# Sums of k and v in linear attention ahead of a softplus feed-forward block: one head at a time for every batch

## The chip, the cores and the metric

The kernel runs on one core of a Trainium2 chip. The metric is the device time of one execution in microseconds (us), median of several runs; lower is better. The engines named below are TensorE (PE for its multiplications, PEld for its weight loads), VectorE (DVE), ScalarE (ACT), GpSimd (POOL) and SyncE (SP), whose queue issues the transfers.

## What is computed

The first part is a linear attention: k and v of each head are summed over the sequence into a 64 x 64 matrix, q is multiplied with it, and each row is scaled by its root mean square. The second part is a feed-forward block with softplus. `w_in` and `w_out` arrive as float64.

```python
# B = 8 batches, H = 8 heads, S = 576 positions, D = 64
kv  = np.einsum('bhsd,bhse->bhde', k, v)          # the sums of k and v
out = np.einsum('bhsd,bhde->bhse', q, kv)
rms = np.sqrt(np.mean(out * out, axis=-1, keepdims=True) + 1e-06)
x   = out / rms * g_norm                          # then (B,H,S,D) -> (4608, 512)
h   = x @ w_in                                    # 512 -> 2048
g   = np.maximum(h, 0.0) + np.log1p(np.exp(-np.abs(h)))
y   = g @ w_out                                   # 2048 -> 512
```

## The kernel before

All work is entered as tasks into a plan, which sorts them before the program is built. A task has an engine, an assumed duration in ns, the tasks that it follows, a position and the buffers that it takes and gives back. Among the tasks that could start at nearly the same time on an engine, the one with the lowest position goes first. The positions come from a list of numbers: those of the first four chunks of weights (converted at `CONVERT`, fetched at `FETCH`), leads of several loads (`EARLY`), and those of the later chunks (`LATER`).

```python
P0 = [-71.0, -4.7, -70.3, -8.7, ...]               # 40 numbers
CONVERT, FETCH, EARLY, LATER = P0[:8], P0[8:16], P0[16:27], P0[27:]
...
def x_pos(t):       # position of a tile of 128 rows
    n = t // TB
    return t * EARLY[0] + EARLY[1] if n == 0 else first_step[0, n] - (EARLY[2] if n == 1 else EARLY[3]) + t % TB
...
def x_again(ph, t):                                # a tile of x is loaded again
    pos = first_step[ph, t // TB] - EARLY[8] + 0.5 * (t % TB)
    ... load at pos - EARLY[9] ...
def leave(ph, t, bank, done, pos):                 # partial results of a former phase
    ... load at pos - EARLY[10] ...
```

The sums of one batch are made in five parts: four of 128 partitions with 4 positions each (the parts p = 0 to 3 hold heads p and p + 4), and the tail, the last 64 positions of all heads. `pairs(x, i)` is two heads side by side, 128 wide. Batches 0 and 1 (`wide_rows`) have the four main parts a head at a time (64 x 64, line 505); everything else multiplies two heads of k with two heads of v (128 x 128, line 513), and only the two diagonal blocks of the product are used later.

```python
def kv_of(b):
    pos = x_pos(first_tile[b]) - (EARLY[4] if b else EARLY[5])
    wide_rows = b < 2
    bank = slot("o")                               # one bank of PSUM
    MAIN = 4 * P
    for p in range(NP + 1):
        tail = p == NP
        ks, vs = (slot(f"tail{i}" if tail else "m") for i in range(2))
        n = S - MAIN if tail else P
        def load(src, s, ...):
            if tail: ...                           # k: two transfers (L483), v: one (L485)
            x = new(s, [P, H, D])
            src = src[b, p::NP, :MAIN].rearrange("h (s i) d -> s h i d", i=4)
            if s is ks and not wide_rows:
                for h in range(2):
                    nc.sync.dma_start(out=x[:, h::2], in_=src[:, h])                              # L491
            else:
                nc.sync.dma_start(out=x.rearrange("s (h i) d -> s h i d", h=2), in_=src)          # L493
        ...
        def run(...):
            kv = new(bank, [P, NP, 2, D]) if p == 0 else bank.tile
            for i in range(4):
                if wide_rows and not tail:
                    for e in range(2):
                        l, r = (x.tile.rearrange("s (h i) d -> s h i d", h=2)[:, e, i] for x in (ks, vs))
                        nc.tensor.matmul(kv[e * D:(e + 1) * D, p, e], lhsT=l, rhs=r, ...)         # L505
                    continue
                ...                                # l: two heads of k, r: two heads of v
                nc.tensor.matmul(kv[:, i if tail else p], lhsT=l, rhs=r, ...)                     # L513
        last = add("PE", 1640 if wide_rows and not tail else 820, run, lds + [last], pos + 0.5 * p, ...)
    # the two diagonal blocks go to kv_diag, whose other blocks stay zero (L520, L521)
```

The product with q (`o`) takes the block-diagonal `kv_diag` and so a pair of heads at a time:

```python
nc.tensor.matmul(y[r0:r0 + n, p::NP], lhsT=qT.tile[:, p, r0:r0 + n],
                 rhs=kv_diag[b % 2][:, p].rearrange("r (h d) -> r h d", d=D), ...)                # L530
```

The rows are then scaled (ACT, DVE, POOL), turned, and split into three parts of fewer bits for the feed-forward block (L437, L440, L444). That block has 192 steps, each of 12 matmuls into `h` (L668) and 9 into `s` (L675), with softplus and the split of its result between them (L688, L690, L679, L683). Where TensorE would have nothing to do before the first step, the plan puts in matmuls whose result isn't used (L784).

Of the kernel before, what the change touches and what calls it, by code (L numbers as in the profile page):

```python
# [18 lines left out]
P = 128  # L19
# [21 lines left out]
class Plan:  # L41
# [13 lines left out]
    def slot(self, ring):  # L55
        return Slot(ring)

    def add(self, engine, ns, run, after=(), pos=0.0, take=(), give=(), size=0, behind=None, follows=None):
        t = Task(engine, ns, run, [a for a in after if a is not None], pos, list(take), list(give), size)
        for s in t.give:  # L60
            s.readers += 1
        self.tasks.append(t)
        t.follows = follows
        t.behind = behind
        return t
# [77 lines left out]
def kernel(  # L143
# [24 lines left out]
    nc = tc.nc  # L168
    B, H, S, D = q.shape
# [3 lines left out]
    NP = H // 2  # L173
# [9 lines left out]
    PLACES = 8  # L183
    LAST = PHASES[-1]

    P0 = [-71.0, -4.7, -70.3, -8.7, -15.1, -0.5, -23.9, 2.7, -65.0, -28.3, -35.2, -10.7, -25.2, 1.3,
          -0.2, -2.7, 0.5, -17.5, 13.0, 9.5, 5.5, 6.5, -2.0, 2.5, 2.5, 28.0, 15.0, 14.5, 8.5, 44.5,
          49.5, 68.5, 52.5, 72.0, 94.5, 99.5, 115.5, 110.5, 114.5, 8.5]
    CONVERT, FETCH, EARLY, LATER = P0[:8], P0[8:16], P0[16:27], P0[27:]
    BY_PE = 12  # L190
    AT_ONCE = 2 * TB
# [22 lines left out]
                 h=2, o=2, tp=1, s0=1, s1=1, s2=1)  # L214
# [3 lines left out]
    slot, add = plan.slot, plan.add  # L218

    def new(s, shape, dtype=F32):  # L220
        pool = ps if s.ring in PS else sb
        s.tile = pool.tile(shape, dtype, tag=f"{s.ring}_{s.place}", name=f"{s.ring}_{s.place}")
        return s.tile

    def pairs(x, p):

        return x[:, 2 * p:2 * p + 2].rearrange("r h d -> r (h d)")


    def halves(src, e):  # L230

        return src[e * NP:(e + 1) * NP].rearrange("p s d -> s p d")
# [224 lines left out]
    kv_ready = {}  # L457
    o_tasks = {}

    def x_pos(t):  # L460

        n = t // TB
        return t * EARLY[0] + EARLY[1] if n == 0 else first_step[0, n] - (EARLY[2] if n == 1 else EARLY[3]) + t % TB

    def kv_of(b):

        pos = x_pos(first_tile[b]) - (EARLY[4] if b else EARLY[5])
        wide_rows = b < 2
        bank = slot("o")
        last = None  # L470
        MAIN = 4 * P
# [5 lines that stand above are left out]
            def load(src, s, p=p, tail=tail, n=n, ks=ks):  # L477
                if tail:
                    s.tile = tails[s is not ks]
                    src = src[b, :, MAIN:]  # L480
                    if s is ks:
                        for e in range(2):
                            nc.sync.dma_start(out=s.tile[:n, e::2], in_=halves(src, e))  # L483
                    else:
                        nc.sync.dma_start(out=s.tile[:n], in_=src.rearrange("h s d -> s h d"))  # L485
                    return
                x = new(s, [P, H, D])
                src = src[b, p::NP, :MAIN].rearrange("h (s i) d -> s h i d", i=4)
                if s is ks and not wide_rows:
                    for h in range(2):  # L490
                        nc.sync.dma_start(out=x[:, h::2], in_=src[:, h])  # L491
                else:
                    nc.sync.dma_start(out=x.rearrange("s (h i) d -> s h i d", h=2), in_=src)  # L493

            lds = [add("SP", ns, lambda src=src, s=s, load=load: load(src, s), (), pos - EARLY[6] + 0.5 * p, [s], [],
                       620 if tail else size, behind=int(pos - 2) - 3)
                   for src, s, ns, size in ((k, ks, *((500, 850) if wide_rows and not tail else (900, 1300))), (v, vs, 500, 850))]

            def run(ks=ks, vs=vs, p=p, tail=tail, n=n):
                kv = new(bank, [P, NP, 2, D]) if p == 0 else bank.tile  # L500
                for i in range(4):
                    if wide_rows and not tail:
                        for e in range(2):
                            l, r = (x.tile.rearrange("s (h i) d -> s h i d", h=2)[:, e, i] for x in (ks, vs))
                            nc.tensor.matmul(kv[e * D:(e + 1) * D, p, e], lhsT=l, rhs=r, start=(p == 0 and i == 0),  # L505
                                             stop=False, skip_group_check=True)
                        continue
                    if tail:
                        l, r = pairs(ks.tile, i), vs.tile[:, i::NP]
                    else:  # L510
                        l, r = pairs(ks.tile, i), vs.tile.rearrange("s (h i) d -> s h i d", h=2)[:, :, i]

                    nc.tensor.matmul(kv[:, i if tail else p], lhsT=l, rhs=r, start=(p == 0 and i == 0), stop=tail,  # L513
                                     skip_group_check=True)
            last = add("PE", 1640 if wide_rows and not tail else 820, run, lds + [last], pos + 0.5 * p,
                       [bank] if p == 0 else [], [ks, vs])
        kvd = kv_diag[b % 2]
        old = o_tasks.get(b - 2, [])
        kv_ready[b] = [
            add("ACT", 360, lambda: nc.scalar.copy(kvd[:D, :, :D], bank.tile[:D, :, 0]), [last] + old, pos + 2.5, [], [bank]),  # L520
            add("ACT", 360, lambda: nc.scalar.copy(kvd[D:, :, D:], bank.tile[D:, :, 1]), [last] + old, pos + 2.5, [], [bank])]  # L521

    def rows(t):
        pos = x_pos(t)
# [235 lines left out]
    for c in range(KF):  # L760
        for j in (2 * c, 2 * c + 1):
            pos = CONVERT[j] if c < 4 else LATER[c - 4] + LATER[12] * (j % 2)
            weight(j, pos, FETCH[j] if c < 4 else pos)
    for b in range(B):
        kv_of(b)
        for t in range(n_tiles):
            if parts(t)[-1][0] == b:
                rows(t)
# [51 lines left out]
```

## Time and profile before

| | |
|---|---|
| time, median of 3 runs | 917.79 us (917.73 to 917.94) |
| span of the profiled run | 917.5 us |
| last matmul ends | 913.6 us |
| sums of k and v, matmul records | 192 + 64 at 128 x 128, 128 at 64 x 64 |
| transfers | 131.44 MB in 230,386 packets, 127,408 of them under 512 bytes |

The profile gives for each engine its busy time. A group of instructions is listed as line, engine, operation, what it writes and reads, its shape and count, then total busy time in us, the mean duration in ns, and how long the engine idled before it. The durations of matmuls overlap one another, so that the time from one group's start to the next one's says more than a duration. "SPq" is the queue that issues transfers.

### The profile page before, as it was taken

The numbers are of one execution on the slowest core, as the hardware profiler recorded it, in microseconds if no ns is written. First come the engines' busy times: TensorE is split into PE (matmuls) and PEld (weight loads), VectorE is DVE, ScalarE is ACT, GpSimd is POOL, SyncE is SP. The second block draws the span as 40 slices with busy tenths as digits, with TensorE's granted clock in tenths as the row PEclk, the third lists the DMA queues.
The fourth block names the chain that finished last, engine by engine and source line by source line (L and its number), as shares of the span: only waits on it lengthen the run. The fifth ranks groups of instructions, "written<-read, shape, count | busy, mean of one in ns | idle before, by whom it ended". The sixth has DMA issues, their size and how long they took to land.

```text
span 917.5 us, 13377 instructions
## 1 busy us (share of the span) xinstructions
PE 898.1 (98%) x4863; PEld 812.4 (89%) x4863; DVE 626.6 (68%) x1055; ACT 415.1 (45%) x799; POOL 81.2 (9%) x78
## 2 busy tenths in 40 slices
PE   5799999999999999999999999999999999999998
PEld 4689999989998999999999999999999999998987
DVE  5877887875457887789856778888444455555553
ACT  4776555444334656455434455446323333333331
POOL 0324421312122100000000000000000000000000
PEclk9999999999999999999999999999999999999999
DMA  7999999397883654445433434643320433333323
GB/s 226 241 224 224 260 207 203 89 216 147 176 139 108 149 150 127 125 139 172 149 104 127 150 126 139 208 142 122 104 70 33 138 102 103 106 104 104 104 69 104
DMA packets 230386, 131.44 MB, mean 143 GB/s; under 512 B 127408, under 2 KB 204208, under 8 KB 230320
## 3 DMA queue, kind: packets, MB, share of 16 engines
q1 hardware_dynamic: 230160, 130.59, 53.7%
q8 instruction: 38, 0.62, 0.3%
q14 instruction: 28, 0.23, 0.1%
q10 hardware_dynamic: 160, 0.00, 0.0%
HBM read 91.75 MB, written 38.80 MB: 142 GB/s over the span
## 4 chain that ended last, share of the span: by engine, by line
PE 95%; DMA 2%; DVE 1%; ACT 1%; SPq 0%; issue 0%; ACTq 0%
PE s L675 44%; PE h L668 43%; PE o L530 3%; PE o L513 3%; DMA m<-in_v_dram 1%; DMA g_col<-in_g_norm_dram 1%; PE tp L547 0%; DMA tail<-in_k_dram 0%; SPq L608 0%; PE o L505 0%; PE h L367 0%; DVE xv L440 0%; DVE xv L444 0%; PE tp L585 0%; ACT L750 0%
## 5 line engine op out<-in xcount | busy, mean ns | idle before, releaser
L668 PE MATMUL h<-xv,w 128*128 128x384 f32 x2304 | 434.3, 337 | 0.9 <-ACT g L688 0.9
L675 PE MATMUL s<-w,gv 128*128 128x512 f32 x1728 | 434.2, 395 | 0.0
L668 PEld LDWEIGHTS h<-xv,w 128*128 128x128 f32 x2304 | 406.6, 188 | 15.9 <-ACT g L688 1.1
L675 PEld LDWEIGHTS s<-w,gv 128*128 128x128 f32 x1728 | 319.4, 188 | 58.9 <-issue 0.5
L688 ACT ACTIVATE g<-h 128x384 f32<-128x384 f32 x192 | 94.3, 491 | 392.7 <-PE h L668 388.2
L679 DVE TENSOR_TENSOR gv<-g,gv 128x384 fp32r<-128x384 f32 x192 | 106.4, 554 | 179.1 <-ACT gv L690 178.2
L690 ACT ACTIVATE gv<-g 128x384 fp32r<-128x384 f32 x192 | 100.9, 525 | 22.9 <-PE s L675 15.6
L683 DVE SCALAR_TENSOR_TENSOR gv<-gv 128x384 fp32r<-128x384 f32 x192 | 106.9, 557 | 6.1
L440 DVE SCALAR_TENSOR_TENSOR xv<-m,g_col,xv 128x512 fp32r<-128x512 f32 x102 | 75.9, 744 | 1.3 <-ACT xv L437 1.1
L444 DVE SCALAR_TENSOR_TENSOR xv<-xv 128x512 fp32r<-128x512 f32 x108 | 74.4, 689 | 2.6
L437 ACT ACTIVATE xv<-m,g_down 128x512 fp32r<-128x512 f32 x102 | 69.5, 710 | 1.1 <-DMA m<-x 1.1
L539 POOL TENSOR_TENSOR r<-r,half 128x8 f32<-128x8 f32 x36 | 65.5, 1818 | 3.0
L715 DVE SCALAR_TENSOR_TENSOR m<-s,scale,m 128x512 f32<-128x512 f32 x24 | 17.9, 747 | 30.1 <-PE s L675 30.1
L530 PE MATMUL o<-kv_diag,m 128*128 128x128 f32 (+1 forms) x296 | 36.9, 275 | 0.0
L530 PEld LDWEIGHTS o<-kv_diag,m 128*128 128x128 f32 (+1 forms) x296 | 35.1, 179 | 2.0 <-issue 1.0
L538 POOL TENSOR_SCALAR r<-r 128x8 f32<-128x8 f32 x36 | 15.1, 419 | 240.9 <-DVE r L535 240.6
L715 DVE SCALAR_TENSOR_TENSOR m<-s,m 128x512 f32<-128x512 f32 x36 | 23.7, 684 | 13.5 <-PE s L675 13.4
L542 DVE TENSOR_TENSOR x<-o,r 128x512 f32<-128x512 f32 x33 | 22.7, 687 | 13.5 <-POOL r L539 13.4
L535 DVE TENSOR_REDUCE r<-x 128x8 f32<-128x512 f32 x36 | 24.5, 680 | 10.2 <-ACT x L598 10.0
L303 ACT ACTIVATE sq<-sq,big 128x512 bf16<-128x512 bf16 x32 | 22.9, 717 | 11.2 <-DVE m L299 11.1
L286 ACT ACTIVATE sq<-raw 128x512 bf16<-128x512 bf16 x32 | 21.2, 664 | 12.5 <-DMA raw<-in_moe_w_in_dram 8.3
L299 DVE SCALAR_TENSOR_TENSOR m<-sq,m 128x512 f32<-128x512 bf16 x32 | 22.1, 690 | 6.3 <-ACT sq L286 4.9
(69 smaller groups left out, 452.8 us busy)
## 6 DMA issues: line engine op xcount, KB each, us to landing
m<-x SPq DMA_DIRECT2D x102, 256.0 KB, 4.7
part<-m SPq DMA_DIRECT2D x72, 256.0 KB, 2.7
m<-part SPq DMA_DIRECT2D x72, 256.0 KB, 3.7
raw<-in_moe_w_in_dram SPq DMA_DIRECT2D x16, 512.0 KB, 5.7
m<-in_v_dram SPq DMA_DIRECT2D x32, 256.0 KB, 4.2
raw<-in_moe_w_out_dram SPq DMA_DIRECT2D x16, 512.0 KB, 5.1
qa<-in_q_dram SPq DMA_DIRECT2D x24, 288.0 KB, 6.3
m<-in_k_dram SPq DMA_DIRECT2D x48, 128.0 KB, 4.1
```

The costliest lines, as they stand in the source:

```text
L437: nc.scalar.activation(cols(0, F32R), x.tile, func=AF.Identity, scale=g_down)
L440: nc.vector.scalar_tensor_tensor(out=cols(1, F32R), in0=x.tile, scalar=g_col, in1=cols(0), op0=ALU.mult, op1=ALU.subtract)
L444: nc.vector.scalar_tensor_tensor(out=cols(2, F32R), in0=cols(1), scalar=-RADIX, in1=cols(0), op0=ALU.mult, op1=ALU.add)
L530: nc.tensor.matmul(y[r0:r0 + n, p::NP], lhsT=qT.tile[:, p, r0:r0 + n], rhs=kv_diag[b % 2][:, p].rearrange("r (h d) -> r h d", d=D), start= ...
L539: nc.gpsimd.tensor_tensor(out=r.tile, in0=r.tile, in1=half, op=ALU.pow)
L668: nc.tensor.matmul(hp, lhsT=w_in.tile[:, i, kd * P:(kd + 1) * P], rhs=xv.tile[:, i, kd], start=(m == 0), stop=(m == 3 * KD - 1))
L675: nc.tensor.matmul(mine[i].tile, lhsT=gv.tile[:, m, i * P:(i + 1) * P], rhs=w_out.tile[:, m], start=(c == cs[0] and m == 0), stop=(c == cs ...
L679: nc.vector.tensor_tensor(out=gv.tile[:, 1], in0=g.tile, in1=gv.tile.bitcast(F32)[:, 0], op=ALU.subtract)
L683: nc.vector.scalar_tensor_tensor(out=gv.tile[:, 2], in0=f32[:, 1], scalar=-RADIX, in1=f32[:, 0], op0=ALU.mult, op1=ALU.add)
L688: a = add("ACT", 490, lambda: nc.scalar.activation(new(g, [P, NT]), h.tile, func=AF.Softplus, scale=1.0 + E), [a], s, [g], [h])
L690: a = add("ACT", 530, lambda: nc.scalar.activation(new(gv, [P, 3, NT], F32R)[:, 0], g.tile, func=AF.Copy, scale=DOWN), [a], s, [gv])
L715: a = add("DVE", 700, lambda: nc.vector.scalar_tensor_tensor(out=new(ot, [P, d_model]), in0=bank.tile, scalar=(scale if ph == LAST else 1. ...
```

## The change

Every batch gets its sums one head at a time, tails too; the wide form goes away. A matmul then makes only the 64 x 64 product that is used, and two heads that write the two halves of the partitions follow each other. The sums of a pair need only one 64-wide column in PSUM instead of two. As k no longer has to lie with two heads side by side, it is loaded as v is: one transfer a part, in runs of 4 positions (1 KB), and the tail of k in one transfer too. The product with q stays with pairs of heads. The plan's assumed durations follow, and the list of positions is chosen anew.

```diff
-    P0 = [-71.0, -4.7, -70.3, -8.7, -15.1, -0.5, -23.9, 2.7, -65.0, -28.3, -35.2, -10.7, -25.2, 1.3,
-          -0.2, -2.7, 0.5, -17.5, 13.0, 9.5, 5.5, 6.5, -2.0, 2.5, 2.5, 28.0, 15.0, 14.5, 8.5, 44.5,
-          49.5, 68.5, 52.5, 72.0, 94.5, 99.5, 115.5, 110.5, 114.5, 8.5]
+    P0 = [-72.5, -0.2, -57.8, -8.7, -11.6, -12.0, -21.4, 2.2, -57.5, -32.8, -36.2, -10.7, -28.2, 0.3,
+          -3.2, -2.2, 0.5, -17.5, 12.5, 9.5, 5.5, 6.5, -2.0, 2.5, 2.5, 33.5, 12.5, 14.5, 8.5, 44.5,
+          49.5, 68.5, 52.5, 73.0, 96.5, 99.5, 115.5, 110.5, 114.5, 8.5]
@@ kv_of, loads
-                    if s is ks:
-                        for e in range(2):
-                            nc.sync.dma_start(out=s.tile[:n, e::2], in_=halves(src, e))
-                    else:
-                        nc.sync.dma_start(out=s.tile[:n], in_=src.rearrange("h s d -> s h d"))
+                    nc.sync.dma_start(out=s.tile[:n], in_=src[b, :, MAIN:].rearrange("h s d -> s h d"))
                     return
-                ... (two transfers of k for batches 2 to 7, as shown above)
+                nc.sync.dma_start(out=new(s, [P, 2, 4, D]), in_=src[b, p::NP, :MAIN].rearrange("h (s i) d -> s h i d", i=4))
@@ kv_of, matmuls
-                kv = new(bank, [P, NP, 2, D]) if p == 0 else bank.tile
+                kv = new(bank, [P, NP, D]) if p == 0 else bank.tile
                 for i in range(4):
-                    ... (both forms, as shown above)
+                    for e in range(2):
+                        l, r = (x.tile[:, i + e * NP] if tail else x.tile[:, e, i] for x in (ks, vs))
+
+                        nc.tensor.matmul(kv[e * D:(e + 1) * D, i if tail else p], lhsT=l, rhs=r,
+                                         start=(p == 0 and i == 0), stop=tail, skip_group_check=True)
-            last = add("PE", 1640 if wide_rows and not tail else 820, run, lds + [last], pos + 0.5 * p,
-                       [bank] if p == 0 else [], [ks, vs])
+            last = add("PE", 600, run, lds + [last], pos + 0.5 * p, [bank] if p == 0 else [], [ks, vs])
@@ kv_of, copies to kv_diag: the same two, from bank.tile[r:r + D]
```

More of the change, by code (lines that the diff above doesn't have):

```diff
@@ L467, in kv_of @@
         pos = x_pos(first_tile[b]) - (EARLY[4] if b else EARLY[5])
-        wide_rows = b < 2
         bank = slot("o")
@@ L479, in load @@
                     s.tile = tails[s is not ks]
-                    src = src[b, :, MAIN:]
-                    if s is ks:
-                        for e in range(2):
-                            nc.sync.dma_start(out=s.tile[:n, e::2], in_=halves(src, e))
-                    else:
-                        nc.sync.dma_start(out=s.tile[:n], in_=src.rearrange("h s d -> s h d"))
-                    return
-                x = new(s, [P, H, D])
-                src = src[b, p::NP, :MAIN].rearrange("h (s i) d -> s h i d", i=4)
@@ L489, in load @@
[L489 to L497, printed above, removed]
@@ L499, in run @@
-            def run(ks=ks, vs=vs, p=p, tail=tail, n=n):
-                kv = new(bank, [P, NP, 2, D]) if p == 0 else bank.tile
-                for i in range(4):
[L502 to L514, printed above, removed]
@@ L515, in kv_of @@
-            last = add("PE", 1640 if wide_rows and not tail else 820, run, lds + [last], pos + 0.5 * p,
-                       [bank] if p == 0 else [], [ks, vs])
+                    nc.sync.dma_start(out=s.tile[:n], in_=src[b, :, MAIN:].rearrange("h s d -> s h d"))
+                    return
+                nc.sync.dma_start(out=new(s, [P, 2, 4, D]), in_=src[b, p::NP, :MAIN].rearrange("h (s i) d -> s h i d", i=4))
+            lds = [add("SP", 500, lambda src=src, s=s, load=load: load(src, s), (), pos - EARLY[6] + 0.5 * p, [s], [],
+                       650 if tail else 850, behind=int(pos - 2) - 3) for src, s in ((k, ks), (v, vs))]
@@ new lines, in run @@
+            def run(ks=ks, vs=vs, p=p, tail=tail):
+                kv = new(bank, [P, NP, D]) if p == 0 else bank.tile
+                for i in range(4):
+                    for e in range(2):
+                        l, r = (x.tile[:, i + e * NP] if tail else x.tile[:, e, i] for x in (ks, vs))
+                        nc.tensor.matmul(kv[e * D:(e + 1) * D, i if tail else p], lhsT=l, rhs=r,
+                                         start=(p == 0 and i == 0), stop=tail, skip_group_check=True)
@@ L517, in kv_of @@
+            last = add("PE", 600, run, lds + [last], pos + 0.5 * p, [bank] if p == 0 else [], [ks, vs])
         kvd = kv_diag[b % 2]
[L518 to L521, printed above, removed]
+        kv_ready[b] = [add("ACT", 360, lambda r=r: nc.scalar.copy(kvd[r:r + D, :, r:r + D], bank.tile[r:r + D]),
+                           [last] + o_tasks.get(b - 2, []), pos + 2.5, [], [bank]) for r in (0, D)]
```

## The prediction

> **What bounds the kernel now.** I read the page first, then busy time by stretch, then the order of instructions on TensorE, then the transfers. The page's totals and its chain of waits come first:
>
> ```profile
> PE 898.1 (98%) x4863; PEld 812.4 (89%) x4863; DVE 626.6 (68%) x1055; ACT 415.1 (45%) x799; POOL 81.2 (9%) x78
> ...
> PE 95%; DMA 2%; DVE 1%; ACT 1%; SPq 0%; issue 0%; ACTq 0%
> ```
>
> TensorE is busy for 98% of the span and holds 95% of the chain that ends last. An average can hide a stage with another limit, so I look at stretches. The columns are the stretch, its length, then busy time and count of PE, PEld, DVE, ACT and POOL, the clock, the DMA share and GB/s:
>
> ```profile
> 0.00:10.00 10.00, 4.78 (x20) 3.12 (x22) 3.45 (x10) 2.22 (x3) 0.69 (x6) 1.00 0.75 233
> 10.00:20.00 10.00, 6.03 (x64) 4.53 (x62) 7.55 (x13) 7.04 (x14) 0.00 (x0) 1.00 0.75 205
> 20.00:30.00 10.00, 8.65 (x71) 6.95 (x70) 8.93 (x16) 8.27 (x18) 2.93 (x4) 1.00 0.99 279
> 30.00:40.00 10.00, 7.31 (x86) 5.99 (x86) 8.41 (x15) 7.69 (x16) 4.90 (x5) 1.00 0.95 227
> 40.00:50.00 10.00, 8.44 (x56) 7.09 (x54) 5.86 (x10) 5.52 (x11) 0.93 (x1) 1.00 0.84 218
> 50.00:60.00 10.00, 9.32 (x64) 8.38 (x63) 8.46 (x15) 6.48 (x15) 2.41 (x2) 1.00 0.90 242
> 60.00:70.00 10.00, 10.00 (x75) 9.49 (x74) 8.31 (x15) 7.81 (x15) 3.47 (x4) 1.00 1.14 193
> ...
> 100.00:150.00 50.00, 50.00 (x292) 45.73 (x291) 42.71 (x73) 28.16 (x55) 12.59 (x11) 1.00 0.97 216
> ```
>
> There are two regimes. Up to about 54 us TensorE has gaps (its last wait before the steady part ends at 53.27 us), while the DMA share is mostly 0.8 to 1.0 and DVE and ACT are each busy for 7 to 9 us of every 10 between 10 and 40 us. From there to 913.6 us TensorE has no gap at all: every row after 60 shows a full 10.00 or 50.00. So **in the second regime time is the sum of TensorE's work**, and a microsecond less of it is a microsecond off the end, unless something else starts to arrive late. In the first regime time is set by loads and by the chain through DVE and ACT.
>
> Which TensorE work does the change touch? Only the sums of k and v. These are the groups by shape; the number ahead of the comma is busy time with overlaps counted once, the next is the mean duration of a record:
>
> ```profile
> L513 PE MATMUL o<-m,m 128*128 128x128 f32 x192 | 24.9, 275 | 0.7 <-DMA m<-in_v_dram 0.7
> L513 PE MATMUL o<-tail,tail 128*128 128x128 f32 x64 | 8.9, 283 | 0.0
> L505 PE MATMUL o<-m,m 128*64 128x64 f32 x128 | 7.0, 272 | 6.8 <-DMA m<-in_v_dram 6.8
> ```
>
> Each fp32 matmul leaves two records: 6 batches x 4 x 4 = 96 matmuls give 192. The kernel already holds both forms. L505, used for batches 0 and 1, is the form that the change puts everywhere: eight 64-wide matmuls a quarter instead of four 128-wide ones of which half the product is unused. So its price can be read off, as long as its early and cold executions are told from its later ones. TensorE in order of time (start, duration, group):
>
> ```profile
> 17.17 1.98 PE L505 MATMUL o<-m,m 128*64 128x64 f32 x32
> ...
> 27.04 0.69 PE L505 MATMUL o<-m,m 128*64 128x64 f32 x16
> 27.65 1.16 PE L530 MATMUL s<-kv_diag,m 128*128 128x128 f32 x8
> ...
> 51.10 1.06 PE L513 MATMUL o<-m,m 128*128 128x128 f32 x8
> 51.99 0.60 PE L585 MATMUL tp<-ident_r,m 128*128 128x128 f32 x4
> ```
>
> From the start of a group to the start of the next one: **0.61 us** for the 64-wide quarter (27.65 - 27.04), **0.89 us** for the 128-wide one (51.99 - 51.10). The chain of waits agrees, with "PE o L513 x8" at 0.89 us a group throughout.
>
> **What the Trainium skill says.** "TensorEngine Tiling (Array Packing)", Overview and Tiling Modes: a 128x64 arrangement gives two tiles that load weights and multiply in parallel, worth up to twice the speed where the stationary side is at most 64 wide; but changing the arrangement drains TensorE. The trace agrees with both halves. Eight matmuls take 0.61 us or 76 ns each, against 0.89 / 4 = 222 ns for a 128-wide one; with half the columns and no overlap, one would expect 111 ns. And the full factor is not there: by columns alone eight at 222 / 4 would be 0.44 us, and they take 0.61, which leaves some 0.17 us a group for starts and changes of arrangement.
> "TensorE: Matmul & The Clock Gate", Part 1: after idling, TensorE runs at half rate until it has been kept busy. Here the two quarters at 17.17 us take 1.91 us to the next start, so 0.95 each, against 0.61 later. That is why I don't use the mean of L505.
> "DMA: Bandwidth & Descriptors", Specifications: pieces under 512 bytes stay below line rate. Whole transfers of k in 256-byte runs (128 KB each) land in a median of 4.1 us, those of v in 1 KB runs (256 KB) in 4.2: half the bytes in the same time. The trace agrees, though both also wait behind other transfers.
>
> **The change, part by part.**
> 1. *Main sums of batches 2 to 7.* Six batches x 4 quarters = 24 groups go from 0.89 to 0.61 us: 0.28 less each. The first two (51.10 and 53.27) lie where TensorE still waits for transfers, so I count 22: 22 x 0.28 = **6.2 us**.
> 2. *Tail sums.* One group of four 128-wide matmuls per batch becomes eight 64-wide ones. Those of batches 0 and 1 (19.67 and 37.98 us) lie in the early regime; six count: 6 x 0.28 = **1.7 us**.
> 3. *Weight loads.* They double in number but are half as wide: L505's load at 158 ns median and L513's at 192 overlap their matmuls. They are already in the 0.61; nothing extra.
> 4. *Copies out of PSUM.* Two copies of 64x256 per batch before and after (353 and 369 ns). Only the stride of the source changes: nothing. They lie on ACT, which is busy 56% in 100 to 150 us.
> 5. *Loads of k, batches 2 to 7.* Two issues of 128 KB in 256-byte runs become one of 256 KB in 1 KB runs. On the queue a pair takes 1.25 us to issue, one load of v 0.45 to 0.57:
>
> ```profile
> 48.04 1.22 SPq L491 DMA_DIRECT2D m<-in_k_dram  x2
> 49.37 0.56 SPq L493 DMA_DIRECT2D m<-in_v_dram  x1
> ```
>
> So about 0.7 us of issue is saved for each of 24 loads, and 0.85 for each tail of k (1.47 for two becomes about 0.61). After 60 us that is hidden: TensorE waits for no transfer there. From 13 to 54 us the queue issues almost without a pause, and the change takes away two tails (1.7 us) and two or three loads of k (1.4 to 2.1 us), over 3 us of issue. But part of an issue's length is the queue being full, and the chain in that stretch also runs through DVE, ACT and the landing of v. I take a third: **1.2 us** off the start of the steady part.
> 6. *Positions chosen anew.* They move the conversions and fetches of the first four weight chunks, the lead of the second block (13.0 to 12.5), and the lead of later loads (28.0 to 33.5, 15.0 to 12.5). They add no instruction. They can move the start of the steady part by a microsecond or two either way. I presume that they were picked for this order of work, and credit **0.6 us**.
>
> Sum: 6.2 + 1.7 + 1.2 + 0.6 = 9.7 us; 917.8 - 9.7 = 908.1. I state **908.3 us**, a fraction kept back for hand-overs in which DVE becomes the later one.
>
> **The rivals.**
> *DVE takes the place of TensorE.* In 100 to 150 us DVE is busy for 42.7 of 50 us, 85%, with the same work to do in less time: 13 groups x 0.28 = 3.6 us fewer in the 90 us after 60 raises that to about 89%. Against it: no wait of TensorE for DVE after 54 us. For it: the order on each engine is fixed, so that one late result stops TensorE. If it bites, half the gain of parts 1 and 2 is lost: 912 to 913 us.
> *Each change of arrangement costs more among the big matmuls.* My 0.61 us is from a group between fp32 groups; in the steady part most neighbours are L668 and L675, in another type. After an L513 group the following L668 chain piece is 2.11 instead of 2.08 us, so a switch of that kind costs little today. A further 0.15 us a group would be 28 x 0.15 = 4.2 us: 912.5. For the opposite case: compared by durations (1.06 against 0.69), a group saves 0.37 us, which makes 28 x 0.37 = 10.4 instead of 7.9 and the time 906.
> *The start decides.* TensorE idles for 19.4 us in the whole span, 3.9 of them after the last matmul, and runs 9.0 us of pure warming (L784). Those and the half-rate stretch are what the start could give. If 256-byte runs and issues truly hold up the start, it could gain 4 us: 905. If the new positions starve it (the first weight fetches are moved by 1 to 7 positions, one conversion by 12), it could lose 4: 913.
> *The transfers were what mattered, and the matmuls are hidden.* Then only part 5 would show, and the time would be about 916. The rows of 10.00 after 60 us speak against it.
>
> **Range and chances.** Parts 1 and 2 give 5 to 10.4 us, the start -4 to +4, and these are independent: 8 in 10 lie within about 5 us of the middle, 903.5 to 913.5. Two per cent is 18.4 us, below 899.4 or above 936.1. Faster by that needs parts 1 and 2 at their best and 8 us from the start, of which it shows about 25 at all: 0.02. Slower by that needs a new stall that the steady part has no trace of: 0.02. Within 2%: 0.96.
>
> **What would show it.** Right: the 256 128-wide records of the sums (192 + 64) are gone and there are 8 batches x 5 groups x 16 = 640 of the 64-wide kind in place of 128; groups at about 0.61 us from start to start in 100 to 280 us; TensorE without gaps from before 54 us; and 24 loads x 1024 runs of 256 bytes become 24 x 256 of 1 KB, so that 24,576 fewer packets lie under 512 bytes and 18,432 fewer in all. Wrong: quarters at 0.75 us and over among L668 and L675 (dear switches); new waits of TensorE for DVE after 60 us; or a first steady stretch that begins more than 3 us earlier or later.

## The result, and the profile after

The changed kernel takes **912.56 us** (912.22 to 913.73, 4 runs) against 917.87 us: ratio 0.9942, 95% interval 0.9925 to 0.9960, a gain of 5.3 us. Predicted were 908.3 us, in a range of 903.5 to 913.5. A second, later measurement gave 0.9944 (0.9931 to 0.9956). The profiled execution of the kernel before was 1.4 us longer than that kernel's median, so the two spans, 917.5 and 910.9 us, differ by more than the medians do.

From the page of the changed kernel, totals and chain of waits:

```profile
PE 898.6 (99%) x5134; PEld 802.6 (88%) x5134; DVE 625.7 (69%) x1055; ACT 414.9 (46%) x799; POOL 80.6 (9%) x78
...
PE 97%; ACT 1%; DVE 1%; DMA 1%; issue 0%; ACTq 0%; DVEq 0%
```

TensorE's busy time has not fallen at all, though the sums need less of it. The groups by shape show where it went:

```profile
L494 PE MATMUL o<-m,m 128*64 128x64 f32 x512 | 22.6, 239 | 3.9 <-DMA m<-in_v_dram 3.9
L762 PE MATMUL h<-ident_r 128*128 128x512 f32 x36 | 15.7, 554 | 1.6 <-DVE ident_r L731 1.6
...
L494 PE MATMUL o<-tail,tail 128*64 128x64 f32 x128 | 5.5, 228 | 0.0
```

The sums went from 40.8 us (three groups) to 28.1, but the matmuls put in to keep TensorE warm went from 21 to 36 (9.0 to 15.7 us). They fill gaps at the start, where the new order leaves TensorE fewer waits: its idle time in the span falls from 19.4 to 12.3 us. These busy times overlap between groups and so don't add up. Counted from each group's start to the next start, without waits, the sums take 8.1 us less (33.8 to 25.7), the warming matmuls 6.2 more, and the steps of the feed-forward block, whose work is unchanged, 1.9 more. Waits fall by 7.3 us, so that waits and warming together, which is what the start could give, fall by 1.1. Stretches of the start (columns as in the prediction):

```profile
30.00:40.00 10.00, 9.39 (x119) 7.07 (x118) 9.10 (x16) 7.70 (x16) 4.59 (x5) 1.00 0.83 214
40.00:50.00 10.00, 9.74 (x72) 8.52 (x68) 9.24 (x16) 9.12 (x19) 4.69 (x4) 1.00 1.03 301
50.00:60.00 10.00, 10.00 (x98) 8.28 (x97) 8.49 (x15) 6.92 (x14) 2.41 (x2) 1.00 0.98 264
```

From 41 us on TensorE has no gap (before: 53.27). The counts came as foretold: 640 records of the narrow kind, 25,087 packets fewer under 512 bytes and 18,941 fewer in all. The tell-tale of the sums is in TensorE in order of time (start, duration):

```profile
53.69 0.69 PE L494 MATMUL o<-m,m 128*64 128x64 f32 x16
54.31 0.98 PE L653 MATMUL s<-w,gv 128*128 128x512 f32 x3
55.21 0.69 PE L494 MATMUL o<-m,m 128*64 128x64 f32 x16
55.83 0.97 PE L653 MATMUL s<-w,gv 128*128 128x512 f32 x3
...
63.32 1.05 PE L508 MATMUL o<-kv_diag,m 128*128 128x128 f32 x8
64.13 0.93 PE L653 MATMUL s<-w,gv 128*128 128x512 f32 x3
64.90 0.60 PE L525 MATMUL tp<-ident_r,x 128*128 128x128 f32 x4
```

A narrow group takes 0.61 or 0.62 us to the next start, as predicted. But three L653 behind it take 0.90 (55.21 - 54.31), and the same three behind a wide group 0.77 (64.90 - 64.13). **Part of the price of a narrow group is booked on its neighbours.** From one narrow group to the next it is 1.52 us; less three L653 at a ninth of 2.09 each, that leaves 0.82 us a group. The chain of waits shows the same. Each piece in it is counted from the end of the piece ahead (start, length). Before:

```profile
265.06 0.89 PE o L513 x8
265.95 2.08 PE s L675 x9
```

After:

```profile
258.24 0.61 PE o L494 x16
258.85 2.28 PE s L653 x9
```

The group became 0.28 us shorter, just as predicted, and the nine matmuls behind it 0.20 us longer, with no wait of TensorE there. A single narrow group is worth 0.08 us.

### The profile page after: what moved, and what is told of

Same layout as the page of the kernel before. It is cut to its first block, busy times and chain, and to the rows that moved or that the text cites. A ratio compares the mean times of both kernels' runs of the same rounds, so it can differ in the third digit from the quotient of the medians.

```text
span 910.9 us, 13889 instructions
## 1 busy us (share of the span) xinstructions
PE 898.6 (99%) x5134; PEld 802.6 (88%) x5134; DVE 625.7 (69%) x1055; ACT 414.9 (46%) x799; POOL 80.6 (9%) x78
## 4 chain that ended last, share of the span: by engine, by line
PE 97%; ACT 1%; DVE 1%; DMA 1%; issue 0%; ACTq 0%; DVEq 0%
PE h L646 44%; PE s L653 44%; PE o L508 3%; PE o L494 2%; DMA g_col<-in_g_norm_dram 1%; PE tp L563 1%; PE h L762 1%; PE tp L525 0%; PE h L367 0%; PE s L508 0%; PE h L366 0%; DVE xv L440 0%; DVE m L351 0%; ACT L728 0%; ACT L727 0%
## 5 line engine op out<-in xcount | busy, mean ns | idle before, releaser
L653 PE MATMUL s<-w,gv 128*128 128x512 f32 x1728 | 434.1, 395 | 0.0
L653 PEld LDWEIGHTS s<-w,gv 128*128 128x128 f32 x1728 | 319.6, 188 | 59.9 <-issue 0.5
L668 ACT ACTIVATE gv<-g 128x384 fp32r<-128x384 f32 x192 | 100.8, 525 | 20.4 <-PE s L653 12.4
L494 PEld LDWEIGHTS o<-m,m 128*64 128x64 f32 x512 | 18.7, 148 | 11.5 <-issue 5.9
```

The source lines that it names most:

```text
L653: nc.tensor.matmul(mine[i].tile, lhsT=gv.tile[:, m, i * P:(i + 1) * P], rhs=w_out.tile[:, m], start=(c == cs[0] and m == 0), stop=(c == cs ...
L668: a = add("ACT", 530, lambda: nc.scalar.activation(new(gv, [P, 3, NT], F32R)[:, 0], g.tile, func=AF.Copy, scale=DOWN), [a], s, [gv])
```

## Experiments

Theory 1: the narrow form saves only about 0.1 us a group among the big matmuls, because entering and leaving its arrangement costs something; the remainder of the gain is in the loads. Rivals: the form saves what I predicted and something gave it back; or the positions made the gain. By "stretch" I mean one or more narrow groups in a row. The kernel before was timed again beside each set of runs: 918.88 us beside experiments 1 to 3, 918.18 beside 4, 918.89 beside 5, against 917.87 above. So ratios count, not differences of us.

**1. Positions alone.** In the kernel before:

```diff
-    P0 = [-71.0, -4.7, ...]      # the list before
+    P0 = [-72.5, -0.2, ...]      # the list after
```

> The kernel before with the new list of positions and nothing else. Theory 1 (the narrow form saves some 4 us in the steady part, and the start gains 1.5 to 3 us, mostly from fewer issues and longer runs of k): the list was chosen for the new durations, so here it brings little, 916.5 to 919. Rival A (the start's gain is all from the positions): 914.5 to 916.5.

Measured: 920.02 us, ratio to the kernel before 1.0012 (1.0003 to 1.0020): not a gain. Of 917.8 us, from which the ranges were reckoned, that makes 918.9, at the upper end of theory 1's. Rival A falls as far as positions alone go.

**2. Everything but the positions.** In the changed kernel the opposite edit.

> The changed kernel with the old list of positions. Theory 1: the form and the loads carry the gain, 912.5 to 914.5. Rival A (positions): 914.5 to 916. Rival B (the new positions cost part of the gain that I predicted): below 911.

Measured: 918.19 us, ratio 0.9987 (0.9979 to 0.9995), or 916.6 reckoned from 917.8. This missed theory 1 and rival A alike: form and loads with the old list bring 0.13%, and the new list a further 0.45%, though alone it costs. Rival B is out as well. The waits of TensorE between 60 and 100 us (waiter, what it waited for, total us, times, longest), where the kernel before and the changed one have none:

```profile
PE tp L525 <- DVE x L520: 1.4, 1, 1.4
PE tp L525 <- ACT w L348: 1.0, 1, 1.0
```

I read this so: with narrow sums TensorE gets ahead, and work of DVE and ACT, still ordered by the old list, comes too late, 2.4 us. The rest of the difference, over 1 us, lies ahead of 60 us and I did not divide it.

**3. Form and loads, each undone in the order of the changed kernel.** Two kernels whose instructions follow each other as in the changed one. The first has the old loads and the old matmuls, the second the old loads with the new matmuls:

```diff
 # first: the kernel before, with the new list and the changed kernel's assumed durations
-    (k, ks, *((500, 850) if wide_rows and not tail else (900, 1300))), (v, vs, 500, 850)
+    (k, ks, 500, 850), (v, vs, 500, 850)                    # and 650 for tails
-    last = add("PE", 1640 if wide_rows and not tail else 820, run, ...)
+    last = add("PE", 600, run, ...)
 # second: the changed kernel, k of batches 2 to 7 in 256-byte runs, its tails in two issues
-    nc.sync.dma_start(out=new(s, [P, 2, 4, D]), in_=src[...])
+    for h in range(2):
+        nc.sync.dma_start(out=x[:, h::2], in_=src[:, h])
+    # and l = ks.tile[:, 2 * i + e]
```

> The matmuls and loads of before (wide form for batches 2 to 7 and all tails, k in 256-byte runs, two issues) in the order of the changed kernel, instruction for instruction. To be compared with the next run, which differs only in the form of the matmuls. Theory 1 (each isolated narrow group costs about 0.82 us among the big matmuls, 0.09 less than a wide one; those in a row 0.48): wide is 4 to 5 us slower than narrow, so 916 to 919. Rival (narrow saves 0.28 us everywhere, and something else gave the gain back): 8 us slower.

> The changed kernel with k of batches 2 to 7 in 256-byte runs and two issues, tails of k in two issues, all in the same order. Theory 1: the loads matter only at the start, 1 to 2 us slower than the changed kernel, 913.5 to 914.5. Rival (transfers are hidden anyway): within 0.4 us of it, 912.2 to 913.

Measured: 919.10 us, 1.0000 (0.9991 to 1.0008), with the old form; 916.53 us, 0.9973 (0.9964 to 0.9982), with the new one. Between these two runs the form is worth 2.6 us (by the intervals, some 1.5 to 3.5): less than theory 1 said and a third of the rival's 8. The loads are worth the step from 0.9973 to 0.9942 or 0.9944, 2.7 to 2.9 us (some 1 to 4.5): more than both expectations.

But 2.6 us is not what the form takes off TensorE's own work, since the run with narrow sums waits for more. The steady part shows this. I count it from the third group of L668's kind (its line differs by kernel) to the last group of all; the order within it is the same in these two kernels and the changed one. It lasts 857.15 us with the old form and old loads, 0.56 of them waits of TensorE; 855.16 with the new form and old loads, 1.92 of them waits; 851.77 in the changed kernel, with no wait. From old form to changed kernel, without the wait, that is 4.8 us. Some 0.4 of these are a delay at one pair of wide groups (2.08 us instead of 1.70), so **the form saves 4.4 to 4.8 us of TensorE's time**, the 4 to 5 of theory 1. Counted from start to next start, the 30 groups of the steady part fall from 25.6 to 17.8 us, by 7.9, and the unchanged work around them rises by 3.1.

The two traces lie beside each other well, as only the form differs. Old form, TensorE and then its weight loads:

```profile
265.61 2.32 PE L676 MATMUL s<-w,gv 128*128 128x512 f32 x9
267.76 1.05 PE L514 MATMUL o<-m,m 128*128 128x128 f32 x8
268.57 1.63 PE L669 MATMUL h<-xv,w 128*128 128x384 f32 x8
```

```profile
267.54 1.08 PEld L514 LDWEIGHTS o<-m,m 128*128 128x128 f32 x8
268.55 1.52 PEld L669 LDWEIGHTS h<-xv,w 128*128 128x128 f32 x9
```

New form, the same place:

```profile
263.19 2.35 PE L670 MATMUL s<-w,gv 128*128 128x512 f32 x9
265.47 0.69 PE L511 MATMUL o<-m,m 128*64 128x64 f32 x16
266.08 1.14 PE L663 MATMUL h<-xv,w 128*128 128x384 f32 x5
```

```profile
263.19 1.92 PEld L670 LDWEIGHTS s<-w,gv 128*128 128x128 f32 x9
265.47 0.55 PEld L511 LDWEIGHTS o<-m,m 128*64 128x64 f32 x16 [0.36 <-issue]
266.08 1.00 PEld L663 LDWEIGHTS h<-xv,w 128*128 128x128 f32 x6
```

Group to next start: 0.81 against 0.61. Nine big matmuls and the group, from the start of the nine to the next start: 2.96 (268.57 - 265.61) against 2.89 us (266.08 - 263.19). Of 0.20 us on the group's own line, 0.07 is left. The weight loads show it at the way in: those of the wide group begin at 267.54, 0.22 us ahead of its first matmul, while the array still multiplies. Those of the narrow group begin with its first matmul, after PEld has stood idle for 0.36 us. On the way out they differ little: the next loads begin 0.02 us ahead of their matmul behind the wide group and with it behind the narrow one. The Trainium skill, "TensorEngine Tiling (Array Packing)", Tiling Modes, Key Properties, says that a change of the arrangement drains TensorE; the idle 0.36 us agrees with this.

And the loads: short runs make TensorE wait in the steady part, where I had called transfers hidden.

```profile
58.68 0.69 PE L511 MATMUL o<-m,m 128*64 128x64 f32 x16 [0.82 <-DMA m<-in_v_dram]
...
62.87 0.69 PE L511 MATMUL o<-m,m 128*64 128x64 f32 x16 [0.90 <-DMA m<-in_v_dram]
```

The named tile is v, which is issued behind k. The lag behind the changed kernel's trace is 1.06 us at the first of these groups of batch 2, 2.9 after these waits, 3.2 at 85 us and 4.4 from 135 us on, where it stays. The last step comes from the queue too. ScalarE's work in both traces, first with short runs, then in the changed kernel:

```profile
126.19 0.66 ACT L287 ACTIVATE sq<-raw 128x512 bf16<-128x512 bf16 x1 [5.67 <-DMA raw<-in_moe_w_in_dram]
```

```profile
118.95 0.68 ACT L286 ACTIVATE sq<-raw 128x512 bf16<-128x512 bf16 x1 [1.62 <-DMA raw<-in_moe_w_in_dram]
```

This load of weights is issued at 119.88 us instead of 113.66, 3 us more than the lag, behind pairs of k that take 1.2 to 1.3 us each on the queue. ScalarE and then VectorE are late, and the weight loads of TensorE wait 0.38 and 0.41 us for VectorE's `gv`. The old form waits 3.53 us for the same load, and TensorE does not feel it.

The first 1.06 us, on the other hand, are not shown to come from the loads. They are all there by 23 us, and two executions of the changed kernel lie 0.76 us apart at 15 us (14.52 and 15.28) and meet again at 22. Nor do these runs tell the length of the runs from the number of issues, which were changed together.

**4. Fewer stretches, and groups twice.** If entering and leaving is what costs, groups in a row must be cheaper. Five groups of a batch as one task, or two and three; and, with the order of all else unchanged, each group done twice:

```diff
-            last = add("PE", 600, run, lds + [last], pos + 0.5 * p, ...)
+            runs.append((run, lds, [ks, vs]))
+            if p in ((4,) if b >= 2 else range(NP + 1)):     # two and three: (1, 4)
+                part_runs = [r for r, _, _ in runs]
+                last = add("PE", 600 if len(runs) == 1 else 480 * len(runs) + 150,
+                           lambda part_runs=part_runs: [r() for r in part_runs], ...)
+                runs = []
 # twice
-                for i in range(4):
+                for turn, i in [(u, i) for u in range(2) for i in range(4)]:
                     ...
-                                         start=(p == 0 and i == 0), ...
+                                         start=(p == 0 and i == 0 and turn == 0), ...
```

> The changed kernel itself, on the chip of the next three runs, as what they are compared with. 912 to 914, 0.994 of the kernel before.

> For batches 2 to 7 the five groups of narrow matmuls of a batch are one task and so follow each other directly; a batch then enters the 64-wide arrangement once. In the changed kernel the 29 groups after 54 us form 24 stretches. Theory 1 (entering and leaving costs 0.34 us a stretch, a further group in a row 0.48): 18 stretches fewer, 6 us less, 906.5 to 909, unless the ten tiles that must be there at once make TensorE wait for transfers. Rival (narrow groups cost the same wherever they stand, and the gain was lost elsewhere): within 1 us of the changed kernel or, with the waits, slower.

> The same with two tasks a batch: two groups, then two and the tail. Here 11 stretches instead of 24. Theory 1: 13 x 0.34 = 4.4 us less than the changed kernel, 908 to 910.5, with fewer waits for transfers than five in a row. Rival: within 1 us of the changed kernel.

> Every group of narrow matmuls is done twice in place, with the order of all else unchanged, so that the sums of k and v come out doubled. A second group follows the first without a change of arrangement. Theory 1: 0.48 us a group, so 29 x 0.48 = 14 us for those in the steady part, and 0 to 4 for those at the start: 926.5 to 932. Rival (a narrow group costs 0.8 us by itself, no matter what stands beside it): 29 x 0.8 = 23 us, 936 and over.

Measured, in this order: 913.64 us; 910.20 us, 0.9917 (0.9902 to 0.9933); 910.11 us, 0.9906 (0.9893 to 0.9920); 928.52 us, 1.0108 (1.0093 to 1.0124).

The steady part is 851.77 us in the changed kernel, 865.77 with groups twice. 14.00 us for 30 groups (one begins before 54 us; the expectations counted 29) is 0.47 us for a group that follows another, the predicted 14. Compare 0.82 for one alone: **0.35 us is the price of standing alone**. The trace of this run shows two in a row, then one big group:

```profile
237.85 1.15 PE L495 MATMUL o<-m,m 128*64 128x64 f32 x32
238.93 2.35 PE L647 MATMUL h<-xv,w 128*128 128x384 f32 x12
```

The pair takes 1.08 us, a single one 0.61; the other 0.20 or so of a border lie in what follows. The steady part with two and three (11 stretches instead of 25) is 847.85 us, 3.9 less, and it has a new wait of 0.7 us for ACT: (3.9 + 0.7) / 14 = 0.33 us a stretch. Five in a row (6 stretches): 849.04 us, 2.7 less, with 3.0 us of new waits: (2.7 + 3.0) / 19 = 0.30. So theory 1 held in its mechanism; five in a row missed its time, by these waits:

```profile
PE h L366 <- ACT g L673: 1.1, 1, 1.1
PE o L495 <- PE h L653: 0.9, 1, 0.9
PE tp L532 <- DVE x L527: 0.8, 1, 0.8
```

**5. Why the narrow form is quicker at all, and the best mix.**

```diff
 # halves apart, in the changed kernel
-                for i in range(4):
-                    for e in range(2):
+                for e in range(2):
+                    for i in range(4):
 # two and three for batch 2, then five in a row
-            if p in ((4,) if b >= 2 else range(NP + 1)):
+            if p in ((4,) if b >= 3 else (1, 4) if b == 2 else range(NP + 1)):
```

> The changed kernel with the eight matmuls of a group in another sequence: first the four that write partitions 0 to 63, then the four that write 64 to 127, instead of by turns. Same matmuls, same order of all else. Theory 1 (the narrow form gains because two halves multiply at the same time; one alone takes 64 / 128 of the 0.222 us of a wide matmul, 0.11): eight take 0.85 instead of 0.47 us, less one overlap where the halves meet, so 30 x 0.3 = 9 us more in the steady part, 921.5 to 925. Rival (a narrow matmul is quick by itself): within 1 us of the changed kernel.

> Batch 2, whose loads are the latest, with two and three groups in a row; batches 3 to 7 with five in a row: 7 stretches instead of 11 (two and three) or 6 (five). Theory 1 at the 0.28 us a stretch that those two runs showed: 4 x 0.28 = 1.1 us less than two and three if no wait comes in, 908.5 to 909.5. If the ten tiles held at once hold up other loads: 910 to 911.

Measured: 920.75 us, 1.0025 (1.0017 to 1.0033), and 908.44 us, 0.9887 (0.9872 to 0.9901). With the halves apart, a group in the steady part:

```profile
166.45 0.97 PE L495 MATMUL o<-m,m 128*64 128x64 f32 x16
167.34 2.34 PE L654 MATMUL s<-w,gv 128*128 128x512 f32 x9
```

0.89 us to the next start instead of 0.61; the steady part is 859.35 us, 7.6 more, 0.25 a group against the 0.3 expected. The matmuls are the same ones; only that writers of the two halves no longer follow each other. The records show the overlap itself: by turns, two of them start 6 or 7 ns apart and the next two 58 ns later (55.320, 55.327 and 55.379 us in the changed kernel), with the halves apart a single one starts every 58 ns. Another cause would be that matmuls in a row then add to the same place in PSUM. It falls with the tails, whose four matmuls of a half write four different places: they take 0.90 us too with the halves apart (65.74 to 66.64). So it is the overlap that makes the narrow form pay, and without it the form would be a loss.

The mix keeps most of both: 7 stretches, 0.9 us of new waits, a steady part of 847.05 us. At 0.9887 against 0.9944 it is 5.2 us quicker than the changed kernel. It beats five in a row (0.9917); its lead on two and three (0.9906) is within the intervals.

## Why the prediction was right or wrong

The time lay inside the range, at its upper end, because the range was wide: 5.3 us of the 9.5 came. The frame held: TensorE's work sets the end after 54 us, and of the rivals it was "each change of arrangement costs more among the big matmuls" that came. That its 912.5 us was met to 0.1 is partly luck: it took 4.2 us from the form, the traces show 3.1, and it kept 1.2 us for loads at the start and 0.6 for positions, which no run shows.

- **Steps 1 and 2, "24 groups go from 0.89 to 0.61 us: 0.28 less each", "six count: 6 x 0.28".** This failed, by size: 4.4 to 4.8 us instead of 7.9. On the line of the 30 groups themselves the 7.9 came in full, and 3.1 us of it was lost on other lines. The 0.61 us was right, but it was read between fp32 groups and from the group's own line, and the cost of the border falls for the greater part on what follows. A group alone saves 0.08 us, not 0.28. I quoted the page on the drain and put all of it into the 0.61. The sign that I had named, groups at about 0.61 us from start to start, came true and could not show this.
- **Step 3, "already in the 0.61; nothing extra".** Wrong for the same reason: the loads of the group's first weights no longer run ahead, and what follows the group takes 0.20 us more.
- **Step 4, copies: nothing.** No wait of TensorE in the changed kernel contradicts it beyond one of 0.3 us at the start; it was not tried by itself.
- **Step 5, loads, 1.2 us off the start.** Too small and in the wrong place: undoing them in the changed kernel costs 2.7 to 2.9 us, and what the traces show of it lies in the steady part (851.77 to 855.16 us). "After 60 us that is hidden" held for the kernel before, at its pace, not for a kernel that got ahead of its loads. Waits and warming at the start fell by 1.1 us in all, and no run divides that between loads, order and sums.
- **Step 6, positions, 0.6 us.** In the sum they gave nothing: with the old form and loads, the new order comes to a ratio of 1.0000. But they are a condition: with the old list, form and loads come to 0.9987. A credit of so many microseconds was the wrong shape for it.
- **The rival "DVE takes the place of TensorE"** was turned down for want of a wait; it is much of what happens with the old list (2.4 us for DVE and ACT), and the new one avoids it.

By the runs, order 0, then form 2.6, then loads 2.7 to 2.9 make up the gain, but they must: each run differs from the next by one step. In another order the shares would differ, because the narrow form without the new loads waits away much of its 4.4 to 4.8 us, while the wide form waits only 0.56 us in the steady part with the old loads. The wide form with the new loads was not run.

## What to carry to other kernels

Price a group of instructions by the distance between two fixed neighbours, not by its own line. In this kernel the narrow arrangement is worth having for several groups at a time and with the halves by turns; scattered singly among wide matmuls it gives back most of what it saves. After one engine is made faster, look again at the order and the loads of the others: here most of the gain was missing with the old order (0.9987 instead of 0.9942), and half of it with the old loads (0.9973).

## What the runs showed of the hardware

- Two fp32 matmuls of 64 columns that write different halves of the partitions run at the same time: 0.47 us for eight by turns in a row. With the halves apart a group took 0.28 us more.
- A stretch of 64-wide matmuls among 128-wide ones costs 0.30 to 0.35 us more than the same matmuls within a stretch. Of this, 0.20 us shows in the nine matmuls behind (2.28 instead of 2.08 us). Its weight loads began with its first matmul, those of a 128-wide group in the same place 0.22 us ahead.
- k of six batches in runs of 256 bytes and two issues each, and the tails of k in two issues, cost 2.7 to 2.9 us of a kernel in which TensorE had shown no gap after 41 us. Run length and issues were not told apart.
